# Attention over a cached K and V: keys loaded for two units at a time in 32 KiB rows, with two K and two V buffers

## The chip, the cores and the metric

The kernel runs on one core of one Trainium2 chip. The metric is the device time of one execution in microseconds (us); lower is better. Engines are named as in the profile: PE (matmul) and PEld (its weight loads), DVE (vector), ACT (scalar), POOL (GpSimd), SP (which issues all the DMAs here). "SPq" is SP's instruction queue.

## The reference

Grouped-query attention of 4 new tokens for each of 8 sequences against a cache of 2048 keys. 32 query heads share 8 K/V heads, 4 to each. No causal mask. All inputs are bf16.

```python
B, Sq, D = 8, 4, 512
Hq, Hkv, Sk, Dh = 32, 8, 2048, 128

def reference(x, k_cache, v_cache, wq, wo):
    q = (x @ wq).reshape(B, Sq, Hq, Dh).transpose(0, 2, 1, 3)
    k = jnp.repeat(k_cache, rep, axis=1)
    v = jnp.repeat(v_cache, rep, axis=1)
    scores = jnp.einsum("bhqd,bhkd->bhqk", q, k) * (Dh ** -0.5)
    p = softmax(scores, axis=-1)
    o = jnp.einsum("bhqk,bhkd->bhqd", p, v)
    return o.transpose(0, 2, 1, 3).reshape(B, Sq, Hq * Dh) @ wo
```

K and V are 33.6 MB each, wq and wo 4.2 MB each.

## The kernel before

The work is cut into 16 **units**. A unit is one sequence b and four of the eight K/V heads (G = 4), so 4 heads x 2048 keys of K and as much of V, 2 MB each. In SBUF a unit's K lies as 128 partitions of 64 keys (C = 64, 16 KiB per partition): partition = head x 32 + s, and each partition holds 64 keys that follow one another. V lies the same way.

What is done for a unit n:

- `load_k`, `load_v` (lines 87 to 102) issue its transfers on SP. K has three places in one tile `k_sb`, V three tiles of a pool. A load waits until the last reader of its place is done. SP issues in program order, so a load that waits holds back all that are behind it. `load_ready` (line 122) issues, at the end of each round of the loop, every load whose place has been read by an instruction already in the program.
- `turn_keys(n, t)` (line 141), t = 0 and 1: DVE transposes half of the keys in blocks of 32 x 32 four-byte words, from `k_sb` to one of three `kt` buffers. A four-byte word is two bf16 values, so one transposed half holds even and odd parts of the head dimension beside each other.
- `scores(n, t)` (line 211): eight matmuls of 512 columns into PSUM (`s_ps`), two halves h of the PE's output rows with four accumulating steps each (two 32-blocks of pairs, even and odd). The moving operand steps through `kt` two bf16 values (four bytes) at a time. The queries lie in `q_bd`, block-diagonal over the four heads.
- `maxima(n)`, `exponentials(n)` (lines 232 and 251): DVE takes the maximum over a PSUM tile (1024 values in each of 128 rows), exchanges the two halves and negates; ACT takes the exponential out of PSUM into `s_sb`, with row sums into `l_sb`.
- `sums(n)` (line 283) on POOL adds the row sums of the two halves; `probs_to_keys(n)` (line 262) transposes `s_sb` on DVE into `p_t` and copies it in eight pieces, four on ACT and four on POOL, into `probs`, with keys on partitions; `inverses(n)` (line 290) is DVE's reciprocal of the sums.
- `values(n, quarter)` (line 297): 32 matmuls in four quarters of eight, V against the probabilities, into `o_ps`. `divide(n)` (line 317) scales the result by the reciprocal on ACT, `finish(n)` (line 327) turns it with one PE matmul (`o_t`) and DVE casts it into `oT`.

Each engine executes in the order of the program. The loop (lines 394 to 433) puts, in round n: the sums of unit n - 1; both transposes of unit n; its scores; `finish` of unit n - 3 between the two score groups; the probabilities of unit n - 1; maxima and exponentials of unit n; all values of unit n - 2 (LAG = 2), and its division. Rounds 2 and 3 also make the second half of the queries (`q_products`, `spread_q`).

Ahead of the loop K of unit 0 is loaded, then wq, x, K of units 1 and 2 in one transfer, V of unit 0 and what `load_ready` allows. x lands in a `kt` buffer. After x: PE turns it, multiplies it with half of wq, and DVE, ACT and POOL spread the result into `q_bd` (lines 151 to 203).

After the loop the weights `wo` (loaded in six pieces of 8, 8, 8, 5, 2 and 1 rows per partition, over wq's place, line 393) are multiplied with the outputs of all units, turned twice (`to_tokens`, `to_wo_rows`), and the result is written out. `wo` is the last thing that SP loads.

Of the kernel before, what the change touches and what calls it, by code (L numbers as in the profile page):

```python
# [14 lines left out]
def kernel(  # L15
# [9 lines left out]
    nc = tc.nc  # L25
# [13 lines left out]
    NT, CT = 2, C // 2  # L39
# [5 lines left out]
    KB, VB, PB, LAG = 3, 3, 2, 2  # L45
# [11 lines left out]
    vpool = ctx.enter_context(tc.tile_pool(name="vpool", bufs=VB))  # L57
# [11 lines left out]
    x_sb = ktpool.tile([128, CT, 2, S, 2], BF16, tag="kt", name="x_sb")  # L69
# [12 lines left out]
    ks = [None] * NU  # L82
    vs = [None] * NU

    k_sb = kpool.tile([128, KB, C, Dh], BF16, name="k_sb")

    def load_k(u, n=1):
        hq, b = units[u]
        nc.sync.dma_start(
            k_sb[:, u % KB : u % KB + n, :, :].rearrange("p b c d -> p b (c d)"),  # L90
            k_cache[b : b + n, G * hq : G * hq + G].rearrange(
                "b g (s c) d -> (g s) b (c d)", c=C
            ),
        )
        for i in range(n):
            ks[u + i] = k_sb[:, (u + i) % KB, :, :]

    def load_v(u):
        hq, b = units[u]
        vs[u] = vpool.tile([128, C, Dh], BF16, tag="v_sb", name="v_sb")  # L100
        of = v_cache[b, G * hq : G * hq + G].rearrange("g (s c) d -> (g s) c d", c=C)
        nc.sync.dma_start(vs[u][:, :, :], of)
# [8 lines left out]
    x_all = x_sb[:T, :, :, :, :].rearrange("q c h s e -> q (c h s e)")  # L111
    nc.vector.memset(x_all, 0.0)  # L112
    nc.sync.dma_start(x_all[::XR, :], x.flatten_outer_dims().rearrange("(a i) d -> a (i d)", i=XR))
    load_k(1, 2)
    loads = [("v", 0)]
    for u in range(3, NU + 2):
        if u < NU:
            loads.append(("k", u))
        loads.append(("v", u - 2))
    loads.reverse()  # L120

    def load_ready(nk, nv):
        while loads:
            kind, u = loads[-1]
            if u >= (nk + KB if kind == "k" else nv + VB):
                return
            (load_k if kind == "k" else load_v)(u)
            loads.pop()

    load_ready(0, 0)  # L130
# [10 lines left out]
    def turn_keys(u, t):  # L141
        kts[(u, t)] = ktpool.tile([128, CT, 2, S, 2], BF16, tag="kt", name="kt")
        nc.vector.transpose(  # L143
            kts[(u, t)][:, :, :, :, :].rearrange("k c h s e -> k (c h s e)").bitcast(FP32),
            ks[u][:, t * CT : (t + 1) * CT, :].rearrange("s c d -> s (c d)").bitcast(FP32),
        )

    for t in range(NT):
        turn_keys(0, t)
# [12 lines left out]
    nc.vector.tensor_copy(out=xT_sb[:, :, :], in_=xtp[:, :, :])  # L162

# [47 lines left out]
    def scores(u, t):  # L211
        hq, b = units[u]
        if t == 0:
            s_pss[u] = psum_s.tile([128, NT, CT // 2, S], FP32, tag="s", name="s_ps")
        for i in range(4):
            k, e = i // 2, i % 2
            for h in range(2):
                nc.tensor.matmul(  # L218
                    s_pss[u][h * NQ : (h + 1) * NQ, t, :, :],
                    lhsT=q_bd[:, hq, k, e, b, :, :].rearrange("k g q -> k (g q)"),  # L220
                    rhs=kts[(u, t)][:, h * CT // 2 : (h + 1) * CT // 2, k, :, e],
                    start=(i == 0),
                    stop=(i == 3),
                )
# [7 lines left out]
    def maxima(u):  # L232
# [5 lines left out]
            in_=s_pss[u][:, :, :, :].rearrange("q t c s -> q (t c s)"),  # L238
# [12 lines left out]
    def exponentials(u):  # L251
# [3 lines left out]
            out=s_sbs[u][:, :, :, :].rearrange("q a s j -> q a j s"),  # L255
            in_=s_pss[u][:, :, :, :].rearrange("q t (a j) s -> q (t a) j s", j=2),
# [40 lines left out]
    def values(u, quarter):  # L297
        if quarter == 0:
            o_pss[u] = psum_o.tile([128, 2, Dh], FP32, tag="o", name="o_ps")
        t, h = quarter // 2, quarter % 2  # L300
        for a in range(CT // 4):
# [3 lines left out]
                lhsT=probs[u % PB][:, h, t * CT // 4 + a, :, :, :].rearrange(  # L305
# [87 lines left out]
    pieces = [(0, 0, 8), (1, 0, 8), (2, 0, 8), (3, 0, 5), (3, 5, 2), (3, 7, 1)]  # L393
    for n in range(NU + LAG):
        w = n - LAG
        if 0 < n <= NU:
            total = sums(n - 1)
        if 0 < n < NU:
            turn_keys(n, 0)
            turn_keys(n, 1)  # L400
        if n < NU:
            scores(n, 0)
        if w >= 1 and n < NU:
            finish(w - 1)
# [74 lines left out]
```

## Time and profile before

| | us |
|---|---|
| runs, median of 3 (lowest to highest) | 185.05 (185.0 to 185.06) |
| the profiled execution, its own time | 185.0 |
| its span, first to last instruction | 183.1 |
| PE busy | 123.2 |
| DVE busy | 121.2 |
| ACT busy | 77.9 |
| POOL busy | 59.3 |
| x has landed, first instruction that reads it | 18.71 |
| first scores start | 25.09 |
| first load of V that waits for values (V of unit 3) issued | 50.76 |
| first matmul of the last values starts | 170.22 |
| the last pieces of wo are used from | 179.04 |

Times in the trace are counted from the start of the span; "L89" is line 89 of the kernel. In a row of the timeline the first number is the start in us, the second how long, then the engine, the line, the operation, the tile written <- the tiles read, how many instructions were merged, and in brackets how long the engine had been idle before and what ended it. In a table by stretch there is the stretch, its length, the busy time of PE, PEld, DVE, ACT and POOL (with instructions), the clock granted to PE (1.00 is full), the share of the DMA engines that was busy and GB/s.

### The profile page before, as it was taken

How to read it: one execution, taken by the hardware profiler on the slowest of the kernel's cores; microseconds unless marked ns; L12 is line 12 of the kernel's file. 1: busy time of each engine (PE TensorE's matmuls, PEld its weight loads, DVE VectorE, ACT ScalarE, POOL GpSimd, SP SyncE). 2: the span in 40 equal slices, each digit the busy share in tenths (PEclk: the TensorE clock that was granted, in tenths of full speed). 3: DMA queues.
4: the chain of work that ended last, by engine and by line, in shares of the span. 5: the costliest groups of instructions: out<-in, count | busy, mean ns of one | idle time of the engine just before them, and what ended most of it. 6: DMA issues, size and time to landing. Idle time of an engine off the chain costs nothing.

```text
span 183.1 us, 2559 instructions
## 1 busy us (share of the span) xinstructions
PE 123.2 (67%) x962; PEld 80.4 (44%) x962; DVE 121.2 (66%) x157; ACT 77.9 (43%) x136; POOL 59.3 (32%) x127
## 2 busy tenths in 40 slices
PE   0000652709997978869396878397776978399993
PEld 0000320303664736647154455256463656268872
DVE  6380027797989899894967768576948594946120
ACT  2000112264547748548154544529281719075030
POOL 8900020343237525415151514224240506056000
PEclk9999999995899999999969699969997599969999
DMA  6989999999999999999999999999999999999991
GB/s 182 497 386 419 426 433 429 433 433 426 429 429 437 429 431 420 438 419 437 426 433 429 433 426 437 422 437 433 426 433 429 429 433 426 433 426 422 426 392 49
DMA packets 5666, 75.70 MB, mean 413 GB/s; under 512 B 628, under 2 KB 788, under 8 KB 1044
## 3 DMA queue, kind: packets, MB, share of 16 engines
q1 hardware_dynamic: 5656, 75.57, 97.1%
q8 instruction: 7, 0.11, 0.2%
q14 instruction: 3, 0.02, 0.0%
HBM read 75.53 MB, written 0.03 MB: 413 GB/s over the span
## 4 chain that ended last, share of the span: by engine, by line
DMA 58%; DVE 23%; PE 13%; issue 1%; SPq 1%; POOL 1%; ACT 0%
DMA k_sb<-in_k_cache_dram 38%; DVE kt L143 17%; DMA wo_sb<-in_wo_dram 12%; DMA x_sb<-in_x_dram 8%; PE s_ps L218 6%; PE o_ps L303 4%; DVE top L236 3%; PE psq L169 2%; DVE x_sb L112 1%; SPq L107 1%; POOL q_bd L195 1%; DVE q_t L189 1%; PE out_ps L385 1%; DVE swapped L228 1%; PE xtp L155 1%
## 5 line engine op out<-in xcount | busy, mean ns | idle before, releaser
L143 DVE STREAM_TRANSPOSE kt<-k_sb 128x2048 f32<-128x2048 f32 x32 | 72.0, 2288 | 17.8 <-DMA k_sb<-in_k_cache_dram 17.8
L218 PE MATMUL s_ps<-kt,q_bd 128*64 128x512 bf16 x256 | 44.3, 477 | 37.5 <-DVE kt L143 34.6
L303 PE MATMUL o_ps<-v_sb,probs 128*128 128x256 bf16 x512 | 62.4, 284 | 0.3 <-ACT oT L341 0.3
L274 ACT COPY probs<-p_t 32x512 bf16<-32x512 bf16 x62 | 38.1, 615 | 52.8 <-DVE r_sb L292 51.7
L303 PEld LDWEIGHTS <-probs 128*128 128x128 bf16 x512 | 50.9, 102 | 15.1 <-issue 6.7
L274 POOL COPY probs<-p_t 32x512 bf16<-32x512 bf16 x63 | 38.6, 613 | 56.6 <-DVE r_sb L292 54.3
L218 PEld LDWEIGHTS <-q_bd 128*64 128x64 bf16 x256 | 16.9, 125 | 55.1 <-issue 24.7
L236 DVE TENSOR_REDUCE top<-s_ps 128x1 f32<-128x1024 f32 x16 | 19.6, 1223 | 16.0 <-PE s_ps L218 16.0
L254 ACT ACTIVATE s_sb<-s_ps,less 128x1024 bf16<-128x1024 f32 x16 | 22.4, 1399 | 10.6 <-DVE less L242 10.4
L228 POOL COPY l_swapped<-l_sb 64x1 f32<-64x1 f32 x32 | 5.8, 181 | 32.0 <-ACT s_sb L254 31.3
L155 PE MATMUL xtp<-ident,x_sb 32*128 32x4 bf16 x32 | 1.2, 169 | 18.7 <-DMA x_sb<-in_x_dram 18.7
L323 ACT ACTIVATE o_sc<-o_ps,r_sb 64x128 f32<-64x128 f32 x28 | 10.1, 362 | 7.5 <-PE o_ps L303 6.8
L264 DVE STREAM_TRANSPOSE p_t<-s_sb 128x512 f32<-128x512 f32 x16 | 11.0, 689 | 1.6 <-ACT s_sb L254 1.6
L195 POOL COPY q_bd<-q_t 32x512 bf16<-32x512 bf16 x6 | 3.8, 626 | 18.7 <-DVE q_t L189 18.6
L180 ACT ACTIVATE q_nat<-psq 128x512 bf16<-128x512 f32 x2 | 1.2, 590 | 20.2 <-PE psq L169 20.2
L155 PEld LDWEIGHTS <-x_sb 32*128 32x128 bf16 x32 | 1.1, 112 | 18.7 <-issue 18.7
L340 PEld LDWEIGHTS o_t<-both,o_sc 128*128 128x128 f32 x30 | 4.9, 205 | 6.1 <-issue 4.8
L136 POOL MEMSET probs<- 128x4096 bf16 x2 | 7.0, 3513 | 0.0
L340 PE MATMUL o_t<-both,o_sc 128*128 128x64 f32 x30 | 6.8, 312 | 0.0
L341 DVE CAST oT<-o_t 128x64 bf16<-128x64 f32 x14 | 2.7, 193 | 4.7 <-PE o_t L340 4.7
L228 DVE COPY swapped<-top 64x1 f32<-64x1 f32 x32 | 4.7, 148 | 0.8
L162 DVE CAST xT_sb<-xtp 128x128 bf16<-128x128 f32 x1 | 0.3, 291 | 7.0 <-PE xtp L155 7.0
(37 smaller groups left out, 46.0 us busy)
## 6 DMA issues: line engine op xcount, KB each, us to landing
v_sb<-in_v_cache_dram SPq DMA_DIRECT2D x16, 2048.0 KB, 23.3
k_sb<-in_k_cache_dram SPq DMA_DIRECT2D x14, 2048.0 KB, 23.5
wq_sb<-in_wq_dram SPq DMA_DIRECT2D x1, 4096.0 KB, 17.2
k_sb<-in_k_cache_dram SPq DMA_DIRECT2D x1, 4096.0 KB, 24.3
wo_sb<-in_wo_dram SPq DMA_DIRECT2D x3, 1024.0 KB, 18.9
wo_sb<-in_wo_dram SPq DMA_DIRECT2D x1, 640.0 KB, 21.9
wo_sb<-in_wo_dram SPq DMA_DIRECT2D x1, 256.0 KB, 22.0
wo_sb<-in_wo_dram SPq DMA_DIRECT2D x1, 128.0 KB, 19.6
```

What stands on the lines that cost most here:

```text
L136: nc.gpsimd.memset(pr[:, :, :, :, :, :], 0.0)
L143: nc.vector.transpose(kts[(u, t)][:, :, :, :, :].rearrange("k c h s e -> k (c h s e)").bitcast(FP32), ks[u][:, t * CT : (t + 1) * CT, :].r ...
L195: engines[g](out=q_bd[rows, hq, :, :, :, g, :].rearrange("w k e b (h s) -> w (k e b) h s", h=rep), in_=q_t[rows, :, :, :, :].rearrange("w ...
L218: nc.tensor.matmul(s_pss[u][h * NQ : (h + 1) * NQ, t, :, :], lhsT=q_bd[:, hq, k, e, b, :, :].rearrange("k g q -> k (g q)"), rhs=kts[(u, t) ...
L228: engine.tensor_copy(out=out[h * NQ : (h + 1) * NQ, :], in_=in_[(1 - h) * NQ : (2 - h) * NQ, :])
L236: nc.vector.reduce_max(out=top[:, :], in_=s_pss[u][:, :, :, :].rearrange("q t c s -> q (t c s)"), axis=AX,)
L254: nc.scalar.activation(out=s_sbs[u][:, :, :, :].rearrange("q a s j -> q a j s"), in_=s_pss[u][:, :, :, :].rearrange("q t (a j) s -> q (t a ...
L264: nc.vector.transpose(p_t[:, :, :, :, :].rearrange("s x g q j -> s (x g q j)").bitcast(FP32), s_sbs[u][:, :, :, :].rearrange("q a s j -> q ...
L274: by[h * G + g](out=probs[u % PB][g * S : (g + 1) * S, h, :, :, g, :], in_=p_t[quad * S : (quad + 1) * S, :, g % 2, :, :].rearrange("s x q ...
L303: nc.tensor.matmul(o_pss[u][:, :, :].rearrange("n j d -> n (j d)"), lhsT=probs[u % PB][:, h, t * CT // 4 + a, :, :, :].rearrange("s j g q ...
L323: nc.scalar.mul(out=to, in_=of, mul=by)
L340: nc.tensor.matmul(o_t[:, :], lhsT=o_scs[u][:, :], rhs=both[:, :], start=True, stop=True)
```

## The change

The transfers:

- A **pair** is two units of neighbouring sequences, 2p and 2p + 1. K is loaded by pairs into one of two tiles of 32 KiB per partition. Each unit's K is now 64 rows of 128 keys (32 KiB in HBM and in SBUF), unit 2p in the even partitions and unit 2p + 1 in the odd ones. A pair takes two transfers of 64 rows.
- V keeps its 128 rows of 16 KiB. It has two tiles instead of three places. V of units 13 and 14 goes to the two halves of a K tile that is free by then. x lands in the first V tile, so V of unit 0 waits for x to be read.
- wo's last piece is cut in 6 and 2 rows, not 5, 2 and 1.

The computing:

- A pair has four transposes (NT = 4), each of 32 of the 128 keys of a partition, the same size as before. `scores(p, t)` still has eight matmuls of 512 columns, now four for each unit of the pair; as a unit has each second partition, the moving operand steps four bf16 values (eight bytes).
- The two units' scores lie in two PSUM tiles that live together. The exponential reads them so that its innermost step alternates between the two PSUM banks of a tile.
- The loop goes over the eight pairs. In round p the values of unit 2p - 2 stand in quarters between the score groups of the pair, those of unit 2p - 1 behind the pair's maxima. The last two pairs are ordered differently. Loads are issued at fixed places at the end of a round.

```diff
--- before.py
+++ after.py
-    NT, CT = 2, C // 2
+    NT, CT = 4, C // 2
+    CP = 2 * C
+    SH = S // 2
     HP = 8
     WR = 8
     NP = Hq // HP
     DH = D // 2
     NU = (Hkv // G) * B
-    KB, VB, PB, LAG = 3, 3, 2, 2
+    KB, VB, PB, LAG = 2, 2, 2, 2
+    NPAIR = NU // 2
...
-    ks = [None] * NU
-    vs = [None] * NU
-
-    k_sb = kpool.tile([128, KB, C, Dh], BF16, name="k_sb")
-
-    def load_k(u, n=1):
+    k_sb = [kpool.tile([128, CP, Dh], BF16, name=f"k_sb{i}") for i in range(KB)]
+    v_sb = [vpool.tile([128, C, Dh], BF16, name=f"v_sb{i}") for i in range(VB)]
+    spare = k_sb[NPAIR % KB]
+    vs = [v_sb[u % VB][:, :, :] for u in range(NU)]
+    for i, u in enumerate((NU - 3, NU - 2)):
+        vs[u] = spare[:, i * C : (i + 1) * C, :]
+
+    def load_k(p):
+        hq, b = units[2 * p]
+        for i in range(2):
+            nc.sync.dma_start(
+                k_sb[p % KB][i::2, :, :],
+                k_cache[b + i, G * hq : G * hq + G].rearrange("g (s c) d -> (g s) c d", c=CP),
+            )
+
+    def load_v(u):
         hq, b = units[u]
         nc.sync.dma_start(
-            k_sb[:, u % KB : u % KB + n, :, :].rearrange("p b c d -> p b (c d)"),
-            k_cache[b : b + n, G * hq : G * hq + G].rearrange(
-                "b g (s c) d -> (g s) b (c d)", c=C
-            ),
-        )
-        for i in range(n):
-            ks[u + i] = k_sb[:, (u + i) % KB, :, :]
-
-    def load_v(u):
-        hq, b = units[u]
-        vs[u] = vpool.tile([128, C, Dh], BF16, tag="v_sb", name="v_sb")
-        of = v_cache[b, G * hq : G * hq + G].rearrange("g (s c) d -> (g s) c d", c=C)
-        nc.sync.dma_start(vs[u][:, :, :], of)
+            vs[u], v_cache[b, G * hq : G * hq + G].rearrange("g (s c) d -> (g s) c d", c=C)
+        )
...
     load_k(0)
     nc.sync.dma_start(wq_sb[:, :, :], wq.rearrange("(p r) n -> p r n", r=R))
-    x_all = x_sb[:T, :, :, :, :].rearrange("q c h s e -> q (c h s e)")
+    x_all = v_sb[0][:T, :, :].rearrange("q c d -> q (c d)")[:, : XR * D]
     nc.vector.memset(x_all, 0.0)
     nc.sync.dma_start(x_all[::XR, :], x.flatten_outer_dims().rearrange("(a i) d -> a (i d)", i=XR))
-    load_k(1, 2)
-    loads = [("v", 0)]
...
+    load_k(1)
...
-    def turn_keys(u, t):
-        kts[(u, t)] = ktpool.tile([128, CT, 2, S, 2], BF16, tag="kt", name="kt")
+    def turn_keys(p, t):
+        kts[(p, t)] = ktpool.tile([128, CT, 2, S, 2], BF16, tag="kt", name="kt")
         nc.vector.transpose(
-            kts[(u, t)][:, :, :, :, :].rearrange("k c h s e -> k (c h s e)").bitcast(FP32),
-            ks[u][:, t * CT : (t + 1) * CT, :].rearrange("s c d -> s (c d)").bitcast(FP32),
-        )
-
-    for t in range(NT):
+            kts[(p, t)][:, :, :, :, :].rearrange("k c h s e -> k (c h s e)").bitcast(FP32),
+            k_sb[p % KB][:, t * CT : (t + 1) * CT, :].rearrange("s c d -> s (c d)").bitcast(FP32),
+        )
+
+    for t in range(3):
         turn_keys(0, t)
...
+    load_v(0)
+    load_v(1)
...
-    def scores(u, t):
-        hq, b = units[u]
+    def scores(p, t):
+        pair = (2 * p, 2 * p + 1)
         if t == 0:
-            s_pss[u] = psum_s.tile([128, NT, CT // 2, S], FP32, tag="s", name="s_ps")
+            for u in pair:
+                s_pss[u] = psum_s.tile([128, 2, CT, SH], FP32, tag="s", name="s_ps")
         for i in range(4):
             k, e = i // 2, i % 2
-            for h in range(2):
+            for j, u in enumerate(pair):
+                hq, b = units[u]
+                h = (t + j) % 2
                 nc.tensor.matmul(
-                    s_pss[u][h * NQ : (h + 1) * NQ, t, :, :],
+                    s_pss[u][h * NQ : (h + 1) * NQ, t // 2, :, :],
                     lhsT=q_bd[:, hq, k, e, b, :, :].rearrange("k g q -> k (g q)"),
-                    rhs=kts[(u, t)][:, h * CT // 2 : (h + 1) * CT // 2, k, :, e],
+                    rhs=kts[(p, t)][:, :, k, j::2, e],
                     start=(i == 0),
                     stop=(i == 3),
...
-            out=s_sbs[u][:, :, :, :].rearrange("q a s j -> q a j s"),
-            in_=s_pss[u][:, :, :, :].rearrange("q t (a j) s -> q (t a) j s", j=2),
+            out=s_sbs[u][:, :, :, :].rearrange("q a w j -> q a j w"),
+            in_=s_pss[u][:, :, :, :].rearrange("q i c s -> q c s i"),
...
-        t, h = quarter // 2, quarter % 2
-        for a in range(CT // 4):
+        h, a0 = (quarter // 2 + u) % 2, quarter % 2 * (C // 8)
+        for a in range(C // 8):
             c = quarter * C // 4 + 2 * a
             nc.tensor.matmul(
                 o_pss[u][:, :, :].rearrange("n j d -> n (j d)"),
-                lhsT=probs[u % PB][:, h, t * CT // 4 + a, :, :, :].rearrange(
+                lhsT=probs[u % PB][:, h, a0 + a, :, :, :].rearrange(
...
-    pieces = [(0, 0, 8), (1, 0, 8), (2, 0, 8), (3, 0, 5), (3, 5, 2), (3, 7, 1)]
-    for n in range(NU + LAG):
-        w = n - LAG
-        if 0 < n <= NU:
-            total = sums(n - 1)
-        if 0 < n < NU:
-            turn_keys(n, 0)
-            turn_keys(n, 1)
-        if n < NU:
-            scores(n, 0)
-        if w >= 1 and n < NU:
-            finish(w - 1)
-        if n < NU:
-            scores(n, 1)
-        if n == 2:
-            q_ps = q_products(1)
-        if n == 3:
+    pieces = [(0, 0, 8), (1, 0, 8), (2, 0, 8), (3, 0, 6), (3, 6, 2)]
+
+    def spread(u):
+        total = sums(u)
+        probs_to_keys(u)
+        inverses(u, total)
+
+    def softmax_top(u):
+        maxima(u)
+        exponentials(u)
+
+    def quarters(u, *which):
+        if u is not None:
+            for quarter in which:
+                values(u, quarter)
+
+    done = None
+    for p in range(NPAIR):
+        last = p == NPAIR - 1
+        one, two = (2 * p - 2, 2 * p - 1) if p else (None, None)
+        if p == NPAIR - 2:
+            two = None
+        if last:
+            one, two = 2 * p - 3, 2 * p - 2
+        for t in range(2):
+            if p:
+                turn_keys(p, t)
+            scores(p, t)
+            if t == 0 and done is not None:
+                finish(done)
+        if p == 1:
+            q_nat = scale_q(q_products(1))
+        if p == 2:
             spread_q(1, q_nat, [by_gpsimd] * G)
-        if 0 < n <= NU:
-            probs_to_keys(n - 1)
-            inverses(n - 1, total)
-        if n < NU:
-            maxima(n)
-            exponentials(n)
-        if n == 2:
-            q_nat = scale_q(q_ps)
-        if w == B + 1:
+        if p == B // 2 + 1:
             to_tokens(0)
-        if w == B + 2:
+        if p == B // 2 + 2:
             to_wo_rows(0)
-        if w >= 0:
-            for quarter in range(4):
-                values(w, quarter)
-            if n >= NU:
-                finish(w - 1)
-            (divide_all if w == NU - 1 else divide)(w)
-        load_ready(min(n + 1, NU), max(w + 1, 0))
-        if n == NU - 1:
-            assert not loads, loads
+        quarters(one, 0, 1)
+        if p:
+            turn_keys(p, 2)
+        scores(p, 2)
+        quarters(one, 2)
+        turn_keys(p, 3)
+        if p == 0:
+            load_k(KB)
+        scores(p, 3)
+        quarters(one, 3)
+        if one is not None:
+            divide(one)
+        softmax_top(2 * p)
+        if last:
+            spread(NU - 3)
+        softmax_top(2 * p + 1)
+        if one is not None:
+            finish(one)
+        if last:
+            quarters(two, 0, 1, 2, 3)
+            divide(two)
+            spread(2 * p)
+        else:
+            spread(2 * p)
+            quarters(two, 0, 1, 2, 3)
+            if two is not None:
+                divide(two)
+            if p != NPAIR - 2:
+                spread(2 * p + 1)
+        done = two
+        if p and p < NPAIR - 2:
+            load_v(2 * p)
+            if p < NPAIR - 3:
+                load_v(2 * p + 1)
+            load_k(p + 2)
+        elif p == NPAIR - 2:
+            load_v(NU - 5)
+            for u in (NU - 4, NU - 3, NU - 2):
+                load_v(u)
+        elif last:
+            load_v(NU - 1)
             for piece in pieces:
                 load_wo(*piece)
+    for w in range(NU - 3, NU):
+        quarters(w, 0, 1, 2, 3)
+        finish(w - 1)
+        (divide_all if w == NU - 1 else divide)(w)
+        if w == NU - 3:
+            spread(NU - 1)
```

More of the change, by code (lines that the diff above doesn't have):

```diff
@@ L56 @@
     kpool = ctx.enter_context(tc.tile_pool(name="kpool", bufs=1))
-    vpool = ctx.enter_context(tc.tile_pool(name="vpool", bufs=VB))
+    vpool = ctx.enter_context(tc.tile_pool(name="vpool", bufs=1))
     ktpool = ctx.enter_context(tc.tile_pool(name="ktpool", bufs=3))
@@ L68 @@
     wq_sb = wpool.tile([128, R, HqDh], BF16, tag="w", name="wq_sb")
-    x_sb = ktpool.tile([128, CT, 2, S, 2], BF16, tag="kt", name="x_sb")
     xT_sb = const.tile([128, R, T], BF16, name="xT_sb")
@@ L110 @@
     nc.sync.dma_start(wq_sb[:, :, :], wq.rearrange("(p r) n -> p r n", r=R))
-    x_all = x_sb[:T, :, :, :, :].rearrange("q c h s e -> q (c h s e)")
+    x_all = v_sb[0][:T, :, :].rearrange("q c d -> q (c d)")[:, : XR * D]
     nc.vector.memset(x_all, 0.0)
     nc.sync.dma_start(x_all[::XR, :], x.flatten_outer_dims().rearrange("(a i) d -> a (i d)", i=XR))
-    load_k(1, 2)
-    loads = [("v", 0)]
[L116 to L130, printed above, removed]
+    load_k(1)
     make_identity(nc, ident[:])
@@ L237, in maxima @@
             out=top[:, :],
-            in_=s_pss[u][:, :, :, :].rearrange("q t c s -> q (t c s)"),
+            in_=s_pss[u][:, :, :, :].rearrange("q i c s -> q (i c s)"),
             axis=AX,
```

## The prediction

> **What bounds the kernel now.** I read four views: the page's DMA rows, the DMA queue's own waits, the timeline of all engines, and a table of clock and busy time by stretch. The page first:
>
> ```profile
> DMA  6989999999999999999999999999999999999991
> ...
> q1 hardware_dynamic: 5656, 75.57, 97.1%
> ```
>
> The one hardware queue that SP feeds is busy from 3 us to the end: the kernel is bound by bytes. The trace's packet records give the rate: a 16 KiB packet takes 0.611 us (4096 of K and V), a 32 KiB packet 1.213 (128 of wq), 8 KiB 0.309, 5 KiB 0.196, 2 KiB 0.084, 1 KiB 0.046. So about 9 ns per packet is fixed and the rest is proportional. One K or V unit is 8 packets on each of 16 engines, 4.9 us; two units of K and V are 19.5 us.
>
> Computing is faster, but not by much. The timeline of two units, early and undisturbed by loads:
>
> ```profile
> 65.07 1.09 PE L218 MATMUL s_ps<-kt,q_bd 128*64 128x512 bf16 x8 [0.53 <-DVE kt L143]
> ...
> 66.09 0.43 PE L340 MATMUL o_t<-both,o_sc 128*128 128x64 f32 x2
> ...
> 67.13 0.19 DVE L341 CAST oT<-o_t 128x64 bf16<-128x64 f32 x1
> 67.23 0.33 SPq L89 DMA_DIRECT2D k_sb<-in_k_cache_dram  x1
> 67.24 0.69 DVE L264 STREAM_TRANSPOSE p_t<-s_sb 128x512 f32<-128x512 f32 x1
> ...
> 68.09 2.57 POOL L274 COPY probs<-p_t 32x512 bf16<-32x512 bf16 x4 [2.75 <-DVE r_sb L292]
> ...
> 68.27 3.67 PE L303 MATMUL o_ps<-v_sb,probs 128*128 128x256 bf16 x32
> 68.38 1.22 DVE L236 TENSOR_REDUCE top<-s_ps 128x1 f32<-128x1024 f32 x1 [0.40 <-PE s_ps L218]
> ...
> 70.11 4.49 DVE L143 STREAM_TRANSPOSE kt<-k_sb 128x2048 f32<-128x2048 f32 x2
> ...
> 74.63 0.33 SPq L89 DMA_DIRECT2D k_sb<-in_k_cache_dram  x1
> ```
>
> K loads leave at 67.23 and 74.63, so a unit takes 7.4 us of computing and a pair 14.8, against 19.5 of transfer. That works because the next unit's two key transposes follow at once on DVE, while exponentials, sums and copies of this one run on ACT and POOL. The clock view shows the other price:
>
> ```profile
> 115.00:119.00 4.00, 1.15 (x11) 0.78 (x8) 2.32 (x2) 1.87 (x4) 0.55 (x3) 0.99 1.01 434
> 119.00:122.00 3.00, 2.96 (x14) 1.26 (x16) 2.56 (x3) 0.00 (x0) 0.00 (x0) 0.50 1.01 431
> ```
>
> First number after the stretch's length is PE's busy time, the third last the granted clock. After 4 us with PE busy 1.15, the clock is 0.50 for about 3.4 us, and the eight score matmuls take 1.92 us instead of 1.10. All such drops here (at 92, 102, 119, 139, 160 us) follow some 3.4 us with PE busy under half.
>
> **The transfers, part by part.** K in 32 KiB rows: 128 packets of 0.611 per engine become 64 of 1.213, 78.2 to 77.6 us: minus 0.6, if the packets run at wq's rate. The end of wo: 5, 2 and 1 rows cost 8 x (0.196 + 0.084 + 0.046) = 2.6 us per engine; 6 and 2 rows, with 0.23 between the neighbours, 2.5: minus 0.1, and four matmuls instead of two behind the last piece give 0.1 back. If the queue never ran dry the profiled 185.0 (span 183.1 and 1.9 around it; median of the runs 185.05) would become 184.4.
>
> **The start: the queue runs dry.** The first K transfer is 4 MB instead of 2, so x lands 8 x (1.213 - 0.611) = 4.8 us later, 18.6 to 23.4. Scores began 6.5 us behind x (25.09), now at 29.9. In the order of the new program:
>
> - Four score groups of pair 0: two at 1.82 (3.63 us for 16 matmuls at the start), then two at 1.10: 35.8. The fourth transpose waits for a kt buffer until 31.7 and ends at 34.0; K pair 2 is issued there.
> - Maxima: 1.82 each (28.76 to 30.58): 37.6 and 39.45. Exponential to sums 1.57, sums on POOL 0.68 (32.25 to 32.93).
> - spread() of unit 0 puts four copies on POOL (2.57, 40.2 to 42.8). The sums of unit 1 stand behind them on POOL, end at 43.45, and DVE waits for them in the reciprocal. Behind that reciprocal stand pair 1's transposes: 43.6.
> - Transpose 2.25, scores at half clock 1.92, the second likewise (50.0), the second half of q 1.9 (51.9), two quarters of values 1.84, scores 1.10, a quarter 0.92, scores 1.10, the last quarter 0.92: values of unit 0 end at 57.8.
>
> Only there may V2 be loaded, for V has two buffers instead of three; SP waits, and V3 and K pair 3 stand behind it, although K's buffer is free some 5 us sooner. The stream in front ends at 23.4 + 9.7 (K pair 1) + 9.8 (V0, V1) + 9.7 (K pair 2) = 52.6. First packets come 2.2 us after an issue (0.73 to 2.98). So 60.1 - 52.6 = 7.5 us dry. Before, V3 left at 50.76 with eight units behind x, a stream to 57.7: no gap.
>
> **The loop: a pair takes longer than its transfer.** DVE's chain for one pair at full clock: transpose 2.25; then finish() of the last unit is now between the first and second transposes, so DVE waits for the first scores 1.10, the o_t matmul 0.43, and casts 0.2, with 0.1 of hand-over: 1.8. Second transpose 2.25. Then PE: scores 1.10, two quarters 1.84, scores 1.10, quarter 0.92, scores 1.10: 6.1, which cover the last two transposes (4.5). Two maxima 3.65. Cast 0.2, p_t 0.69, POOL's four copies 2.57, sums 0.68, reciprocal 0.15 and hand-over: 4.3. Together 20.4, against 14.8 before and 19.5 of transfer. PE's values of the odd unit end some 2 us before that; with the next transpose PE has over 4 us of idle, a burst of 1.5, and 2.5 more idle: less than half of any 3.4 us, so by the rows above the clock halves in every pair. That costs 0.8 on the second scores, 1.8 on two quarters, and half of the time 0.8 on the first or third: 3.1, sum 23.5. The bounds are 20.4 (no drop) and 27 (half clock throughout: four score groups and three quarters, 6.5 more); I take 23.5 as the clock view shows drops of one window mostly.
>
> V2 leaves at 57.9, and five pairs later V12: 57.9 + 5 x 23.5 = 175.4. The last pair has one spread before it, not two: maxima 3.65 and p_t 1.0, two transposes 4.5, PE's chain 6.1 at full clock, 8.7 with the drop: 17 with the last quarter, values of unit 11 end at 192.4. From there ACT is last: less 1.0, exponential 1.57, copies of 13 (2.55), exponential 1.57, division 0.76, copies of 14 (2.55), values of 14, finish, values of 15 (3.67 + 0.43 + 3.67): 17.8. What follows the last values took 173.87 to 183.1 before: 9.2. Span 175.4 + 17.0 + 17.8 + 9.2 = 219.4, time 221.3. V15 leaves near 192.4 and wo has landed 17.1 us later (2.2 + 4.9 + 10.0), at 209.5, behind which 3 us remain: the transfers no longer set the end.
>
> **Operations the trace doesn't show.** Keys read eight bytes apart (before four): between nothing and double (1.10 to 1.92 per group); I take nothing, as the four-byte read streams 512 columns for a pair of matmuls in 0.27, hardly over twice the 0.115 of 256 contiguous ones. The Trainium skill (SBUF — State Buffer, Specifications) says that two reads in a 16-byte line still run at full rate: by it the sum stays 221; no run shows it. The exponential now alternates between two PSUM banks: 1.39 to double; I take 1.39, as the strided read of q takes 0.59 for 512 elements. K written to every second partition: between wq's rate and half of it; I take wq's, the only 32 KiB row.
>
> **Rivals.**
> - The clock stays up, or DVE's chain is about 1 us shorter. Then 3.1 x 5 and 2.6 in the last pair fall away: 203; with a pair under 19.5 only the dry start is left, 184.4 + 7.5 = 192. For it: from 125.7 to 129.1 us PE was busy only 1.7 and the clock stayed. Against: the 4 us hole.
> - Strided reads cost double: 2 us more per pair on PE's path, 235; the exponential alone at double, 228. Nothing in the trace speaks for it.
> - The change doesn't do what it says: each K transfer writes 64 partitions, and engines meet at a write port. K at half rate adds 16 x 4.9 = 78 us to a queue that is full: 262. For it: no transfer of before writes every second partition; against it: x, to 4 partitions eight apart, has 0.309 per 8 KiB like wo. The Trainium skill (SBUF — State Buffer, Door 1: The DMA port swizzle) gives 64 adjacent partitions half the ports; even ones by its formula reach all 16, but two engines could still meet at one. No trace here shows the engine of a row.
> - Not slower: computing keeps ahead of the queue. It decides at one place, V2's issue: at 50.4 or sooner nothing runs dry and 184.4 follows. For it: a pair's DVE work is only 14.7 of 19.5. Against: the sums of unit 1 behind POOL's copies, 7 us too late in my working.
>
> **How the numbers follow.** Forecast 221.3 (its own range 211 to 232) 0.58; clock or chain better (192 to 211) 0.18; strided reads 0.09; K at half rate 0.10; not slower 0.05. 192 to 238 leaves out the last two and a little more. Slower 0.95, faster 0.04, within 0.2% (what a measurement here can tell) 0.01.
>
> **What would show it.** Right: the DMA row falls below 9 near 53 to 60 us and then once per pair; SP waits for PE's values ahead of nearly every V; DVE idles ahead of kt and of r_sb; the granted clock is 0.5 in a stretch of each pair; K packets of 32 KiB take 1.213. Wrong: a DMA row of nines from 60 us on (rival one), score groups over 1.5 us at full clock (two), K packets near 2.4 (three), V2 issued ahead of 50.4 (four).

## The result, and the profile after

The changed kernel takes 228.39 us (median; 227.65 to 230.3) against 185.06 for the one before: ratio 1.2352 (1.2307 to 1.2398). The profiled execution took 228.5, its span 226.4, at a mean granted clock of 0.879. Forecast were 221.3 and a span of 219.4.

The page of the changed kernel, with its slices of 5.66 us and the queue's share:

```profile
PEclk9999999557997999889995699559995995999999
DMA  7999999990099968998599929995699929979960
...
q1 hardware_dynamic: 4504, 75.57, 81.5%
```

The row of nines is gone. Two slices, 50.9 to 62.3 us, hold almost no transfer, and after them a hole returns in about every fourth slice, once per pair. The bytes are the same 75.57 MB; the queue that set the end before now has time to spare. What the engines wait for stands in the list of waits (engine, line, what was waited for: us in total, times, longest):

```profile
DVE top L226 <- PE s_ps L208: 37.1, 8, 6.0
DVE oT L331 <- PE o_t L330: 20.4, 7, 3.6
...
DVE r_sb L282 <- POOL l_total L277: 12.5, 7, 2.0
...
DVE kt L128 <- DMA k_sb<-in_k_cache_dram: 8.4, 1, 8.4
```

and, for SP's queue alone:

```profile
SPq L101 <- PE o_ps L293: 141.4, 12, 22.9
```

A load of V waits for PE's values twelve times, 141.4 us in all. In the other direction there is one wait only, for the very first K: from round 1 on, no transpose waits for K and no values wait for V. DVE's longest wait, 37.1 us in eight times, is that of the maxima for the score groups; in the kernel before it was 16.0. It also loses 20.4 us ahead of `finish`'s cast and 12.5 ahead of the reciprocal, seven times each: the two places that the working of the loop named.

One pair in the timeline, from its first key transpose to that of the next pair, 68.09 to 92.05 = 23.96 us:

```profile
68.09 2.31 DVE L128 STREAM_TRANSPOSE kt<-k_sb 128x2048 f32<-128x2048 f32 x1
...
70.54 1.96 PE L208 MATMUL s_ps<-kt,q_bd 128*64 128x512 bf16 x8 [4.62 <-ACT probs L264]
...
73.16 0.23 DVE L331 CAST oT<-o_t 128x64 bf16<-128x64 f32 x1 [2.77 <-PE o_t L330]
73.31 2.30 DVE L128 STREAM_TRANSPOSE kt<-k_sb 128x2048 f32<-128x2048 f32 x1
...
75.66 1.94 PE L208 MATMUL s_ps<-kt,q_bd 128*64 128x512 bf16 x8 [2.53 <-DVE kt L128]
...
77.53 1.92 PE L293 MATMUL o_ps<-v_sb,probs 128*128 128x256 bf16 x16
...
79.38 1.97 PE L208 MATMUL s_ps<-kt,q_bd 128*64 128x512 bf16 x8
...
81.29 1.05 PE L293 MATMUL o_ps<-v_sb,probs 128*128 128x256 bf16 x8
...
82.27 1.90 PE L208 MATMUL s_ps<-kt,q_bd 128*64 128x512 bf16 x8
...
84.20 1.22 DVE L226 TENSOR_REDUCE top<-s_ps 128x1 f32<-128x1024 f32 x1 [3.61 <-PE s_ps L208]
85.18 5.15 SPq L101 DMA_DIRECT2D v_sb<-in_v_cache_dram  x2
...
91.97 0.16 DVE L282 RECIPROCAL r_sb<-l_total 128x1 f32<-128x1 f32 x1 [1.91 <-POOL l_total L277]
```

Read down the start times. Transpose, scores, o_t and cast follow one another (to 73.31), then the second transpose (to 75.6), then five stretches of PE without a break (75.66 to 84.20), then the maxima, and at the end the reciprocal behind POOL. What hides behind this stretch of PE is two transposes, no more. V is issued at 85.18, when the last quarter of values has ended. What the working did not have is the duration of the score groups: four times 1.90 to 1.97. The clock over the second and third of them (columns as before, the clock third from the end):

```profile
75.50:79.00 3.50, 3.34 (x22) 1.74 (x22) 3.50 (x4) 0.00 (x0) 2.41 (x4) 1.00 1.01 433
79.00:82.00 3.00, 3.00 (x20) 1.21 (x18) 1.58 (x1) 0.00 (x0) 0.00 (x0) 1.00 1.10 464
```

It is 1.00. The values prove the same: 1.92 for sixteen matmuls and 1.05 for eight, as in the kernel before. At that clock a score group took 1.09 before, with four-byte steps. So 1.9, which before was a sign of half clock, is here the group's time at full clock. The first group of the same pair, 1.96 us at 70.54, ran at half clock and took no longer:

```profile
70.54:72.50 1.96, 1.96 (x9) 0.63 (x9) 0.00 (x0) 0.51 (x1) 0.04 (x1) 0.50 1.02 418
```

### The profile page after: what moved, and what is told of

It is laid out like the page before. It is cut to its first block, busy times and chain, and to the rows that moved or that the text cites. A ratio compares the mean times of both kernels' runs of the same rounds, so it can differ in the third digit from the quotient of the medians.

```text
span 226.4 us, 2556 instructions
## 1 busy us (share of the span) xinstructions
PE 139.6 (62%) x962; PEld 77.9 (34%) x962; DVE 122.2 (54%) x157; ACT 77.3 (34%) x136; POOL 59.1 (26%) x127
## 3 DMA queue, kind: packets, MB, share of 16 engines
q1 hardware_dynamic: 4504, 75.57, 81.5%
## 4 chain that ended last, share of the span: by engine, by line
PE 51%; DVE 22%; ACT 12%; DMA 9%; POOL 3%; issue 2%; ACTq 0%; POOLq 0%
PE s_ps L208 25%; PE o_ps L293 18%; DVE kt L128 10%; DMA v_sb<-in_x_dram 9%; ACT probs L264 8%; DVE top L226 6%; ACT s_sb L244 3%; PE o_t L330 2%; ACT o_sc L313 2%; PE out_ps L375 2%; DVE swapped L218 2%; PE psq L156 2%; POOL probs L264 1%; DVE less L232 1%; DVE v_sb L113 1%
## 5 line engine op out<-in xcount | busy, mean ns | idle before, releaser
L208 PE MATMUL s_ps<-kt,q_bd 128*64 128x512 bf16 x256 | 61.9, 621 | 53.4 <-ACT probs L264 28.4
L293 PEld LDWEIGHTS <-probs 128*128 128x128 bf16 x512 | 49.2, 100 | 23.1 <-issue 16.8
L293 PE MATMUL o_ps<-v_sb,probs 128*128 128x256 bf16 x448 | 55.4, 278 | 0.0
L208 PEld LDWEIGHTS <-q_bd 128*64 128x64 bf16 x256 | 16.3, 130 | 81.1 <-issue 65.7
L226 DVE TENSOR_REDUCE top<-s_ps 128x1 f32<-128x1024 f32 x16 | 19.5, 1218 | 37.1 <-PE s_ps L208 37.1
L140 PE MATMUL xtp<-ident,v_sb 32*128 32x4 bf16 x32 | 1.2, 169 | 23.9 <-DMA v_sb<-in_x_dram 23.9
L331 DVE CAST oT<-o_t 128x64 bf16<-128x64 f32 x14 | 3.1, 219 | 20.4 <-PE o_t L330 20.4
L330 PE MATMUL o_t<-both,o_sc 128*128 128x64 f32 x30 | 7.5, 338 | 6.1 <-ACT o_sc L313 6.1
L330 PEld LDWEIGHTS o_t<-both,o_sc 128*128 128x128 f32 x30 | 5.5, 230 | 12.3 <-ACT o_sc L313 8.1
L140 PEld LDWEIGHTS <-v_sb 32*128 32x128 bf16 x32 | 1.1, 112 | 23.9 <-issue 23.9
L282 DVE RECIPROCAL r_sb<-l_total 128x1 f32<-128x1 f32 x16 | 2.5, 156 | 12.5 <-POOL l_total L277 12.5
L293 PE MATMUL o_ps<-k_sb,probs 128*128 128x256 bf16 x64 | 7.3, 272 | 0.1
```

What stands on the lines that cost most here:

```text
L208: nc.tensor.matmul(s_pss[u][h * NQ : (h + 1) * NQ, t // 2, :, :], lhsT=q_bd[:, hq, k, e, b, :, :].rearrange("k g q -> k (g q)"), rhs=kts[( ...
L226: nc.vector.reduce_max(out=top[:, :], in_=s_pss[u][:, :, :, :].rearrange("q i c s -> q (i c s)"), axis=AX,)
L293: nc.tensor.matmul(o_pss[u][:, :, :].rearrange("n j d -> n (j d)"), lhsT=probs[u % PB][:, h, a0 + a, :, :, :].rearrange("s j g q -> s (j g q)"
L330: nc.tensor.matmul(o_t[:, :], lhsT=o_scs[u][:, :], rhs=both[:, :], start=True, stop=True)
```

## The experiments

The theory held first that the engines' chain of a pair is longer than its transfer, and that order, clock and reads make it so; the rival, that the dry queue at the start, or one of these parts alone, makes the time. Ratios below are against the kernel before, on the same chip.

**Reads of four bytes, e1.** The scores take the moving operand four bytes apart.

```diff
-    rhs=kts[(p, t)][:, :, k, j::2, e],
+    rhs=kts[(p, t)][:, j * SH : (j + 1) * SH, k, :, e],
```

> The scores read kt[:, 16j:16j+16, k, :, e], four bytes apart as before, instead of kt[:, :, k, j::2, e], eight bytes apart: as many columns and instructions, but the keys of both units are mixed, so the output is not the reference's. Theory A (a pair's chain of computing sets the time, and the eight-byte read costs 0.85 us per group of eight score matmuls at full clock): groups of 1.10 us wherever the clock is full, those in a low-clock stretch stay at 1.9; 1.7 to 3.4 us less per pair, over seven pairs and the start: 203 to 216 us. Theory B (the groups of 1.9 us are the halved clock, as the prediction had it, and the step of the read costs nothing): groups stay near 1.9, 226 to 230 us.

218.19 us, 1.1793 (1.1744 to 1.1843): 10.2 less than 228.39, outside both expected ranges. PE's timeline:

```profile
72.12 1.92 PE L208 MATMUL s_ps<-kt,q_bd 128*64 128x512 bf16 x8 [2.53 <-DVE kt L128]
73.97 2.64 PE L293 MATMUL o_ps<-v_sb,probs 128*128 128x256 bf16 x16
76.54 1.06 PE L208 MATMUL s_ps<-kt,q_bd 128*64 128x512 bf16 x8
```

Two groups of a pair drop to 1.06. Two stay at 1.92, and with them the quarters take 2.64 instead of 1.92: that is the halved clock, forecast for this place. The table by stretch has it over the first of the rows above, 0.50:

```profile
72.12:74.04 1.92, 1.92 (x9) 0.70 (x9) 1.92 (x2) 0.00 (x0) 1.24 (x3) 0.50 0.91 393
```

Pairs take 23.3 us (V issued at 57.72 and, three pairs later, 127.58), against 24.5 (61.20 and 134.59). The eight-byte read costs 10.2 us of the whole; with it gone, the halved clock comes out from under it.

**finish behind both transposes, e2.**

```diff
+        if p:
+            turn_keys(p, 0)
+            turn_keys(p, 1)
         for t in range(2):
-            if p:
-                turn_keys(p, t)
             scores(p, t)
```

> Both first transposes of a pair are put ahead of the scores, so finish() of the last odd unit no longer stands between them on DVE. Theory A (DVE's chain): DVE idles 2.5 to 2.8 us ahead of the cast in rounds 2 to 6 now; that goes, and PE's 2.5 us of idle ahead of the second score group with it: 2.5 x 5 = 12 us less, 216 us. Rival (the transfers, each V waiting for its place, set the pace): loads wait as before, 226 to 230 us.

214.2 us, 1.1578 (1.1544 to 1.1611): 14.2 less. Pairs take 21.6 us (V at 61.03 and 125.96). It is the largest single part, 2.9 us per pair: the second transpose no longer stands behind scores, o_t and cast.

**POOL's sums ahead of its copies, e3.**

```diff
-    def spread(u):
-        total = sums(u)
+    def spread(u, total=None):
+        total = total or sums(u)
...
+            ahead = [sums(2 * p + i) for i in range(2 if p != NPAIR - 2 else 1)]
-            spread(2 * p)
+            spread(2 * p, ahead[0])
...
-                spread(2 * p + 1)
+                spread(2 * p + 1, ahead[1])
```

> POOL makes the sums of both units of a pair ahead of the copies of the even one. Theory A: DVE's wait for the sums of the odd unit (12.5 us over 7 times, 1.9 each) goes, and the next pair's first transpose starts that much sooner: 11 to 13 us less, 215 to 218 us. Rival: the copies of the even unit start 1.3 us later and PE waits for them, so the gain is given back: 226 to 230 us.

218.44 us, 1.1807 (1.1619 to 1.1995): 10 less, just past the upper edge of what was expected, and the interval is wide. The wait is gone from the list:

```profile
DVE r_sb L282 <- POOL l_total L277: 1.0, 1, 1.0
```

12.5 us in seven waits became 1.0 in one. Pairs take 22.9.

**Two more places for V, e4.** V of units 2, 3, 6, 7 and so on goes to the two halves of the tile that holds wq, and later wo. Loads of V no longer wait for the values of the pair in hand.

```diff
+    for u in range(NU - 4):
+        if u % 4 >= 2:
+            place = wo_sb[:, u % 2 * 16 : u % 2 * 16 + 16, :]
+            vs[u] = place.rearrange("p a (b d) -> p (a b) d", d=Dh)
...
             q_nat = scale_q(q_products(1))
+            load_v(2)
+            load_v(3)
```

> V gets two more places, in the room of wq that is free between the second half of q and wo: V of units 2 and 3 is issued behind the second q_products instead of behind the values of units 0 and 1, and all later loads of V one round sooner; the computing is unchanged. Theory A (computing sets the time; from round 1 on no transpose waits for K and no values wait for V): the queue is no longer dry at 53 to 63 us, and the time stays, 226 to 230 us. Rival (the dry queue is what the change costs): 7.5 us or more less, 198 to 221 us.

229.22 us, 1.2389 (1.2259 to 1.252): no change. V2 left at 53.03 instead of 61.20. The page:

```profile
DMA  7999999994999987998599949993899999552000
```

The hole at the start shrinks from two empty slices to one half-filled, and the transfers end some three slices before the kernel does. The time stays. So the dry queue at the start costs nothing here, where computing takes longer than the transfers: feeding the queue sooner only makes the data wait.

**Keys sorted by the transpose, e5.** The transpose writes the words of even and of odd partitions to two blocks, so that the scores read four bytes apart and the layout of K stays.

```diff
-    kts[(p, t)] = ktpool.tile([128, CT, 2, S, 2], BF16, tag="kt", name="kt")
+    kts[(p, t)] = ktpool.tile([128, CT, 2, 2, SH, 2], BF16, tag="kt", name="kt")
...
-            kts[(p, t)][:, :, :, :, :].rearrange("k c h s e -> k (c h s e)").bitcast(FP32),
+            kts[(p, t)][:, :, :, :, :, :].rearrange("k c h j w e -> k (c h j w e)").bitcast(FP32).rearrange("k (a j w) -> k a w j", j=2, w=SH),
...
-    rhs=kts[(p, t)][:, :, k, j::2, e],
+    rhs=kts[(p, t)][:, :, k, j, :, e],
```

> The transpose on DVE writes the words of the even and of the odd partitions to two blocks of kt (kt is [128, CT, 2, 2, SH, 2], written through a view with the two block indices exchanged), so the scores read four bytes apart and the keys are those of the units. Theory A (the eight-byte read is what PE pays, not the layout in HBM): 218 us as in e1, transposes still 2.3 us each. Rival: the scattered write makes the transpose as much slower as the read was, 225 us or more.

241.13 us, 1.3021 (1.2968 to 1.3074): the rival's side. The transposes in the list of groups:

```profile
L128 DVE STREAM_TRANSPOSE kt<-k_sb 128x2048 f32<-128x2048 f32 x32 | 113.2, 3612 | 11.6 <-DMA k_sb<-in_k_cache_dram 8.5 <-PE s_ps L208 3.2
```

3612 ns each, where an unscattered one takes some 2.3 us: the cost moved from PE's reads to DVE's writes, and DVE is on the chain.

**Three repairs together, e6 (e5, e2 and e3), and with places and earlier loads, e7.** In e7, e4's places join, K of pair p + 2 is issued right behind the fourth transpose of pair p, and the second half of q moves to round 0. Of e7's edit, the part that is new:

```diff
-        if p == 0:
-            load_k(KB)
+        if p < NPAIR - KB:
+            load_k(p + KB)
         scores(p, 3)
+        if p == 0:
+            q_nat = scale_q(q_products(1))
+            load_v(2)
+            load_v(3)
```

> e5's write, e2's order and e3's order together; buffers and loads as in the change. Theory A: the gains add until the pair's chain falls under its transfer of 19.5 us; worked forward from the rows, V loads leave 17.5 to 19 us apart, the queue is dry only at the start (5 to 6 us from 52.6) and briefly later, 190 to 195 us. Rival (something else in the new order holds the pair at 20 us or more): 200 us or more.

> e6 and four V places as in e4, the second half of q moved into round 0 so that these places are free at some 40 us, and K of pair p + 2 issued right behind the pair's last transpose. Theory A: with the chain under 19.5 us and no load waiting, the transfers set the end again and the 32 KiB rows show what they bring: 184.4 us, bounds 184 to 187. Rival (32 KiB rows to every second partition bring nothing or the chain still runs over in low-clock pairs): 186 to 195.

214.11 us, 1.1562 (1.1539 to 1.1585), and 213.53, 1.1533 (1.1509 to 1.1558). Both miss, by 19 and by 26 us against the upper end of what was expected, and e7 brings less than 1 us over e6. With transposes of 3.6 us a pair still takes 21.5 us in e6 (V issued at 59.53 and, three pairs later, 123.95), more than its transfer, and loading sooner doesn't help; e9 tests that.

**The kernel before, with eight-byte reads, e8.** The reverse of e1, in a kernel whose queue never runs dry.

```diff
-    rhs=kts[(u, t)][:, h * CT // 2 : (h + 1) * CT // 2, k, :, e],
+    rhs=kts[(u, t)][:, :, k, h::2, e],
```

> The kernel before, with only the scores' read changed to kt[:, :, k, h::2, e], eight bytes apart; as many columns, but the keys of the two halves h are exchanged among each other, so the output is not the reference's. Theory A (the step costs PE 0.85 us per group whatever the kernel): groups of 1.9 to 2.0 at full clock instead of 1.10, and as a unit's computing of 7.4 us becomes 8.3 to 9.2, under its 9.8 of transfer, the time stays within 1 us of 185.05. Rival: groups stay at 1.10 at full clock (then the 1.9 of the change is due to something else, such as two units' outputs interleaved).

185.14 us, 0.9997 (0.9988 to 1.0007): the same. PE's timeline:

```profile
68.69 1.90 PE L218 MATMUL s_ps<-kt,q_bd 128*64 128x512 bf16 x8
70.52 3.67 PE L303 MATMUL o_ps<-v_sb,probs 128*128 128x256 bf16 x32
```

1.90 for the scores, and behind them values at 3.67 for 32, the full-clock figure of before. The eight-byte read alone makes the group 0.8 us longer, in either kernel. Here it is hidden under the transfer; in the changed kernel it is on the chain.

**Both orders and the places, without the scattered write, e9.** e7 without e5's edit.

> e7 without the scattered write of the transpose: e2's and e3's orders, four V places, the second half of q in round 0, scores read eight bytes apart as in the change. Theory A (in-order chain; the scattered write cost e5 to e7 1.3 us in each of 32 transposes): transposes back at 2.3 us; a pair's chain is 9.0 of transposes and, beyond them, PE's values between the score groups, 19.3 at full clock and 21 with a low-clock stretch, against 19.5 of transfer: 190 to 202 us. Rival (the three repairs do not add): 210 us or more.

201.22 us, 1.0868 (1.0843 to 1.0892), within what was expected. Against e7 the difference is the scattered write alone: it costs 12.3 us net, though it frees the scores of the eight-byte read. K now leaves every 19.7 us (52.39 and, four pairs later, 131.12), about the transfer of 19.5.

**Values behind the scores, e10.** In rounds 1 to 6 the values of both units of the last pair stand behind all four score groups, `divide` behind the exponentials, `finish` behind the maxima.

```diff
+        late = one is not None and not last
...
+            if t == 0 and last:
+                for u in pending:
+                    finish(u)
...
-        quarters(one, 0, 1)
+        if not late:
+            quarters(one, 0, 1)
...
+        if late:
+            for u in pending:
+                finish(u)
+            quarters(one, 0, 1, 2, 3)
+            divide(one)
```

> e9 with the values of both units put behind all four score groups of the pair in rounds 1 to 6, their divisions behind the exponentials and both finishes of the last pair behind the maxima. Theory A: DVE then waits for score groups alone; with four groups of 1.95 the chain is 2.3 + 7.8 + 3.7 of maxima + 2.9 to the last reciprocal = 16.7 us, under the transfer of 19.5, so the transfers set the end, with K packets of 1.213 us: 184.4 us, bounds 184.0 to 187, and the scores still take 1.9 a group. Rival (32 KiB rows to every second partition, or two large K places, lose more than the 0.6 us they bring): 185.5 us or more.

192.84 us, 1.0414 (1.04 to 1.0428). The pair did come down to what was worked out, 16.9 against 16.7 us (K issued at 69.97 and, three pairs later, 120.77), below its transfer. The time missed the expected 184 to 187 and lies on the rival's side, 185.5 or more. The page's row of transfers:

```profile
DMA  6999999999999999999999999999999899999400
```

The queue is full from 3 us to about 179 again, but the span is 190.8. SP's issues of K for the last two pairs, in the timeline:

```profile
103.74 1.12 SPq L95 DMA_DIRECT2D k_sb<-in_k_cache_dram  x2
...
120.77 1.12 SPq L95 DMA_DIRECT2D k_sb<-in_k_cache_dram  x2
```

and DVE's first transposes of the last pair:

```profile
150.89 4.50 DVE L129 STREAM_TRANSPOSE kt<-k_sb 128x2048 f32<-128x2048 f32 x2 [4.33 <-DMA k_sb<-in_k_cache_dram]
```

With two places, K of the last pair can be issued only at 120.77; it lands at 150.89, DVE has waited 4.33 us for it, and 40 us of computing stand behind. That fits the second half of the rival, two large places for K; that it is all of the loss was not shown. The transfers of V and wo end some 12 us ahead of the end. The bytes take 177.0 us per DMA engine, against 177.8 in the kernel before: that 0.8 is what the larger rows and wo's cut bring together, and no order run here collects it. Whether K of the last pair, loaded ahead of V10 and V11, would land soon enough was not run.

**Unread matmuls against the clock, e11 (with e1's reads) and e12 (with the eight-byte reads).** PE gets work that nobody reads in its idle places.

```diff
+            if p > 1 and t == 0:
+                keep_busy(32)
             scores(p, t)
...
                 finish(done)
+                keep_busy(16)
```

> e1 (scores read four bytes apart, keys of both units mixed) with matmuls whose result nobody reads in PE's two idle stretches of rounds 2 to 6: 32 of 256 columns ahead of the first score group, 16 behind finish(). Theory A (the clock drop of each pair comes from PE's idle, and costs 3 us of a pair's 23.3 in e1): the clock stays full, all groups take 1.10, loads of V leave 20.4 to 21 us apart in rounds 2 to 6, 201 to 208 us against e1's 218.2. Rival (the clock falls for another reason, or the fill pushes the scores back by as much): 214 us or more.

> The change as it is (eight bytes apart) with the same fill. Theory A (with eight-byte reads a group takes 1.9 to 2.0 at full clock as at half, so the clock has little left to take): groups stay at 1.9 to 2.0 with the clock full, V loads stay 23 to 24.5 us apart, 223 to 230 us against 228.4. Rival (part of the 1.9 is the halved clock): groups fall towards 1.1 and the time by more than 8 us, under 220.

e11 took 201.22 and 204.41 us in two executions, too far apart for an interval; the profile is of the longer one, so what is read from it rests on one trace. PE's timeline in it:

```profile
68.08 1.07 PE L208 MATMUL s_ps<-kt,q_bd 128*64 128x512 bf16 x8 [1.11 <-ACT probs L264]
...
72.05 1.09 PE L208 MATMUL s_ps<-kt,q_bd 128*64 128x512 bf16 x8 [0.79 <-DVE kt L128]
```

The four groups of this pair are at 1.06 to 1.12, and a pair takes 20.3 us (V at 58.76 and, three pairs later, 119.66), where e1 took 23.3. So the halved clock costs 3.0 us per pair where reads are four bytes apart, and it comes from PE's idle, as filling that idle takes it away.

e12 took 224.79 us, 1.2147 (1.2111 to 1.2182), only 3.6 less than without the filling. Its clock by slices:

```profile
PEclk9999999557999999999999999999999999999999
```

and PE's timeline:

```profile
75.04 1.90 PE L208 MATMUL s_ps<-kt,q_bd 128*64 128x512 bf16 x8 [0.79 <-DVE kt L128]
76.87 1.92 PE L293 MATMUL o_ps<-v_sb,probs 128*128 128x256 bf16 x16
```

Full clock from 56 us on, and the group still takes 1.90. Pairs take 23.7 us (V at 60.90 and, three pairs later, 131.93), 3.4 more than in e11: four groups by 0.85. A group takes 1.9 at half clock in e1 and 1.9 at full clock here; the two losses do not add up, they cover each other.

## Why the prediction was right, and where it was wrong

The forecast was slower, at 221.3; it came out slower, 3.2% above that. Step by step, from the trace of the changed kernel:

| step | predicted | measured | added to the span |
|---|---|---|---|
| x is read | 23.4 | 23.88 | |
| scores of the first pair end | 35.8 | 37.6 | |
| first transpose of pair 1 | 43.6 | 45.31 | |
| V2 issued | 57.9 | 61.20 | +3.3 |
| V2 to V12, five pairs | 117.5 | 123.1 | +5.6 |
| last pair | 17.0 | 17.4 | +0.4 |
| values 11 to values 15 | 17.8 | 15.9 | -1.9 |
| behind the last values | 9.2 | 8.8 | -0.4 |
| sum | 219.4 | 226.4 | +7.0 |

**The transfers** were right. K packets of 32 KiB take 1.213 us (median), wq's rate, so K at half rate is refuted. Larger rows and wo's cut were to bring 0.7 together; they bring 0.8 per engine (177.8 to 177.0) in e10, whose queue stays full. In the changed kernel itself the packets took 184.5 (81.5% of the span): by its packet records K's averaged 1.232 us and V's 0.667 (median 0.611), and why they took longer there stays open.

**That a pair takes longer than its transfer** was right, and it is the cause: 24.6 against 19.5, in places that e2 (finish between the transposes, 14.2 us), e3 (sums behind the copies, 10 us) and e10 (values between the scores, 8.4 us against e9) took away. With all of them gone, more places for V and earlier loads, a pair takes 16.9 and the queue is full.

**The dry queue at the start** was found in its place (V2 at 61.20, two empty slices), but it is no cause of its own: e4 fills it and the time stays. The sum needed no price for it, because the chain of computing runs through the same points. What the first rival gave for it, 7.5 us where a pair is shorter than its transfer, stays untested: no run has a short pair and a dry start.

**The eight-byte reads, taken as nothing, are the step that failed.** The bounds given were 1.10 and 1.92 per group; the measured 1.90 to 2.0 at full clock (e8, e12, and the changed kernel itself) lie at the upper end, 0.85 above the value taken. On the chain that is 3.4 us in each pair (e12 against e11), and two groups in the first pair and two in the second, where 1.10 had been worked with, some 3.2 us ahead of V2, the most of the table's +3.3 (in e1 V2 leaves 3.5 us sooner). e1 puts the whole at 10.2 us. The prediction's own sign for this, score groups over 1.5 us at full clock, was there. The argument for nothing was the time of the four-byte reads before, and that says nothing of reads eight bytes apart. The Trainium skill (SBUF — State Buffer, Specifications) asks for two hits in each line of 16 bytes for full bandwidth; eight-byte steps have two, and by that rule the group would have stayed at 1.1. The traces do not agree, at least for PE's moving operand.

**The clock's 3.1 us per pair** was right in size and cause where the reads are four bytes apart (3.0, e11 against e1), though not in its terms: there two groups lose 0.85 each and two quarters 0.7, where 0.8 for one group, half of that for a second and 1.8 for the quarters had been written. (The bound of 27 adds up to 26.4 from its own terms, four times 0.82 and three times 0.92; nothing rests on it.) In the kernel as it was changed, the loss is hardly there: filling PE's idle brings 0.8 us per pair (24.5 to 23.7) and 3.6 in all, where the first rival had 18 for a clock that stays up, as the groups with eight-byte reads take 1.9 at either clock. So the 23.5 forecast for a pair, near the measured 24.6, holds 20.4 that was right (20.3 in e11) and a surcharge of 3.1 that was not far off in size, but for the most part of another origin than written. That the pair came out this near is luck: the loss that was left out covers the one that was counted.

**The tail** was worked out with ACT as last, 17.8 us. PE was, with 15.9: values of units 12 to 15 follow one another at 3.66 each from 202.86 to 217.6, and copies and exponentials are ready in time. The exponential's change of banks costs nothing (1.39 to 1.41).

Of the rivals, strided reads at double cost were true as a mechanism for the scores and wrong in their price, 235, since they were added to the clock's loss; the exponential at double, priced at 228, did not happen, near as that number lies to the result. "Not slower" fell at the place named for it: V2 left at 61.20, not by 50.4.

Still open is why reads eight bytes apart run at about half rate. In the changed kernel and in e8 the two matmuls that share a step (j or h of 0 and 1) read alternate words of the same rows, in e1 and in the kernel before separate blocks: the step and the interleaving always changed together, and which of them costs the time was not told apart. (In e5 they alternate in blocks of 16 words, read four bytes apart, and a group takes 1.06.) The parts of e9 (places, load order, q in round 0) were not told apart either.

## What to carry to other kernels

Before joining two units in one round, add up the round's in-order chain on every engine, short helpers and engine-to-engine waits included, and set it against the round's transfer: a kernel bound by bytes has only that difference to spend, and filling the queue sooner doesn't help once the chain is longer. A changed access pattern is to be measured by itself, in a kernel where it is hidden and one where it is not, rather than taken from a neighbouring pattern. Two losses on the same instruction need not add up, so measure each with the other taken away.

## What the runs showed of the hardware that was not expected

- Eight matmuls of 512 bf16 columns take 1.9 to 2.1 us with a moving operand in steps of eight bytes (the changed kernel, e8, e12), 1.06 to 1.13 in steps of four (e1, e11), both at a granted clock of 1.00. The first two or three groups of a run are left out: they take 1.9 with either step. At half clock the four-byte groups take 1.92 (e1), and the eight-byte ones 1.92 to 1.96 (the changed kernel).
- A 128x2048 fp32 stream transpose on DVE takes 3.61 us where it sorts alternate words into two blocks, and about 2.3 where it doesn't.
- K to every second partition, 64 rows of 32 KiB, runs at the packet rate of wq's 128 rows, 1.213 us by the median. The Trainium skill (SBUF — State Buffer, Door 1: The DMA port swizzle) has the reachable ports depend on bits of the partition number; by its formula even partitions reach all, and the packet time measured agrees with that.
- Some 48 matmuls per pair whose result is never read made e1's kernel 14 to 17 us faster, 218.19 to 204.41 and 201.22; in its trace the clock stays full over these pairs.
